# A new order table for an adaLN transformer block on one core: TensorE's instruction fetches enter the planner's transfer model

## The chip, the cores and the metric

The kernel runs on one core of one Trainium2 chip. The core has five engines with an instruction stream each: TensorE (PE in the profile; its weight loads are PEld), VectorE (DVE), ScalarE (ACT), GpSimd (POOL) and SyncE (SP), which here issues most of the DMAs. The metric is the device time of one execution in microseconds (us). Lower is better.

## The reference

A block of 2048 tokens of width 640 is computed: modulation vectors from a condition `c`, sliding-window attention (32 heads of 20, window 256) and a gated MLP of inner width 1536, each behind a LayerNorm and with a gate on its way back into `x`.

```python
mod = (_silu(c) @ w_mod).reshape(c.shape[0], 6, 1, -1)
sa, ca, ga, sb, cb, gb = (mod[:, i] for i in range(6))
h = _layernorm(x) * (1 + ca) + sa
qkv = h @ wqkv                                  # 32 heads of 20
scores = q @ k^T * 20 ** -0.5, masked to 0 <= i - j < 256
x = x + ga * (softmax(scores) @ v) @ wo
h = _layernorm(x) * (1 + cb) + sb
x = x + gb * ((_sigmoid(h @ w_gate) * (h @ w_up)) @ w_down)
```

## The kernel before

The tokens are cut into 8 chunks of 256 (two blocks of 128). A chunk a goes through these steps:

- **ln1**: two blocks of x are loaded (`load_x`). DVE takes their statistics (`bn_stats`, line 751), POOL takes the power -0.5 (lines 756 and 758), and DVE or POOL writes the normalised rows (lines 768 and 771). They are transposed into hT, by TensorE for chunks 0 and 1, by two transposing DMAs ("atr", issued by SP, line 778) for the others. Five "modulate" operations (one for each 128 columns; line 786 on ACT, 787 on DVE or POOL) multiply by 1 + ca and add sa.
- **qkv**: for each block and each of q and k, two matmul chains of 5 x 320 columns into a PSUM bank, two copies (lines 850 on ACT, 851 on DVE) into a staging tile stg of which there are four, and a transpose into QT or KT: by TensorE for chunks 0 and 1, by one transposing DMA of SP ("qkt") for the others. v needs the copies alone.
- **attention**: 12 score sets (6 in chunk 0). A set is a group of matmuls into the one score tile S (four PSUM banks), one exp of 128x2048 on ACT (line 971), and one or two masks on POOL (979, 981). After six sets their product with v (the lines 657 with M<-E,V) goes to two of the four PSUM banks of M; DVE transposes, divides and transposes back (1018 to 1027), four DMAs write the result to a DRAM tile doc, one DMA per half reads it back as oT.
- **outproj, mlp**: product with wo (its rows times the gate: five DVE or POOL multiplications "wos", line 1192), residual, second LayerNorm, two transposing DMAs ("btr") into h2T, five modulates, then the 12 gate and up chains, tanh on ACT, one DVE product each, and the product with wd.

The first stretch also loads all weights (q, k, v, wo, wg, wu, wd and w_mod) and computes the modulation vectors. For that a small matmul ("ctr") turns c into a column; DVE, ACT and DVE make silu(c) of it (lines 624, 625, 626 and 628, the last being the broadcast copy silubc); "modA" is the product with the first two sixths of w_mod in five steps as the five pieces of w_mod land. "warm" and "fill" are matmuls on zeros whose results nobody uses (lines 637 and 648).

**What sets the order.** The block is not scheduled by the compiler. `Prog.op` numbers 2102 operations as the program is built, each with the engines that may run it, its tiles and a duration. `PLAN` is one list of 2102 numbers: number // 5 is the operation, number % 5 the engine (0 PE, 1 ACT, 2 DVE, 3 POOL, 4 SP). `schedule` walks through the list, gives each operation to its engine's queue in that order, and computes a start time by a model. The modelled times reach the program in one way alone: where a tile needs one of several buffers, it takes the one that the model says is free first. `emit` then writes each engine's queue in order, with the semaphore waits that the dependences need. So an engine runs strictly in the table's order, and an operation that waits holds up all that stand behind it on its engine.

In `schedule`, DMAs go through one modelled pipe: `bw` is the time at which the pipe is free; a DMA starts at the earliest `dlat` after its issue, adds its `work`, and lands 0.83 us before `bw`. `MIXED` is added when transposing and plain DMAs follow each other. `QMAX` holds an issue back when the pipe is over 4.5 us behind.

Of the kernel before, what the change touches and what calls it, by code (L numbers as in the profile page):

```python
# [80 lines left out]
class Prog:  # L81
# [69 lines left out]
    def schedule(self):  # L151
        free = {e: 0.0 for e in ENGS}
        bw = 0.0
        lastturn = False
        order = {e: [] for e in ENGS}
# [37 lines left out]
        for code in PLAN:  # L193
            o, e = self.ops[code // 5], ENGS[code % 5]
            assert e in o.engs and all(d.done for d in o.deps), (o.tag, e)
            st = max(free[e] + (SWITCH if e == "pe" and o.mode != pemode else 0.0), o.tmin)
            for d in o.deps:
                st = max(st, d.end + (0.0 if d.eng == "pe" and o.engs == ("pe",) else d.lat))
            if e == "dve" and o.port:
                st = max(st, free["pool"])  # L200
# [20 lines left out]
            if o.isdma:  # L221
                turn = o.dlat > 3.0
                wait = bw - st - o.dlat
                bw = max(st + o.dlat, bw + (MIXED * min(1.0, wait) if turn != lastturn and wait > 0 else 0.0)) + o.work
                lastturn = turn
                o.end = max(bw - 0.83, st + dur)
                s = rr
                rr = (rr + 1) % NDMA
                dmacnt[s] += 16
                o.key, o.val = f"d{s}", dmacnt[s]  # L230
                if dmalast[s] is not None:
                    o.deps.append(dmalast[s])
                dmalast[s] = o
            else:
                o.end = st + dur
# [104 lines left out]
def c_pe(n):  # L340
# [4 lines left out]
    222, 263, 3, 33, 81, 62, 114, 91, 13, 89, 8, 265, 195, 202, 57, 206, 212, 217, 225, 104, 99, 109, 119, 230, 372,  # L345
    352, 367, 357, 377, 362, 383, 388, 392, 235, 240, 245, 250, 270, 280, 255, 397, 400, 67, 410, 420, 417, 290, 406,
    275, 426, 445, 129, 452, 285, 300, 310, 317, 430, 435, 458, 461, 442, 472, 477, 466, 124, 305, 295, 595, 495, 500,
    480, 485, 580, 507, 520, 492, 134, 23, 526, 139, 144, 149, 742, 585, 591, 38, 530, 535, 73, 541, 154, 510, 516,
    545, 550, 556, 560, 566, 600, 169, 610, 606, 630, 570, 1209, 1214, 747, 762, 757, 752, 767, 617, 635, 642, 576,
    620, 626, 48, 43, 1605, 1611, 773, 778, 645, 787, 660, 650, 782, 667, 680, 685, 790, 796, 657, 710, 692, 820, 827,  # L350
    78, 1620, 1237, 810, 1626, 817, 715, 722, 695, 700, 800, 806, 725, 730, 1222, 736, 1217, 1618, 830, 837, 174,
    1635, 1641, 159, 164, 179, 189, 349, 1514, 18, 53, 1633, 1227, 1232, 1242, 1100, 707, 670, 677, 840, 845, 855,
    1248, 851, 1253, 1267, 1122, 1107, 1705, 1711, 1648, 28, 1718, 1532, 324, 905, 910, 917, 890, 895, 1537, 870, 877,
    901, 860, 1720, 1726, 1542, 867, 1650, 1662, 1657, 194, 930, 937, 920, 1667, 1279, 1134, 1509, 940, 1735, 1258,
    1263, 945, 990, 880, 1733, 926, 995, 952, 334, 970, 1114, 1274, 1672, 887, 955, 960, 1741, 184, 976, 2785, 1677,
    339, 966, 1748, 1288, 1002, 1699, 1005, 1010, 1040, 1045, 344, 1126, 2791, 1020, 1026, 1017, 1517, 1522, 1527,
    1052, 1055, 2805, 2811, 1030, 1085, 1090, 1303, 2798, 1548, 1553, 1558, 1060, 1066, 1291, 1037, 1097, 1567, 1282,
    1750, 1563, 2823, 2825, 1762, 1340, 1757, 1767, 1297, 1070, 980, 1075, 2831, 986, 1772, 1175, 1197, 1082, 2845,
    2851, 1345, 1352, 2684, 1320, 1325, 1139, 1375, 2818, 1119, 1182, 1332, 2843, 1475, 1777, 1694, 1689, 1684, 2689,
    1574, 1390, 2865, 2871, 2838, 2863, 1380, 1387, 1480, 1355, 1152, 2858, 1360, 1486, 1367, 1157, 1395, 1402, 2878,  # L360
    1969, 2885, 1305, 2891, 2883, 1310, 1317, 2707, 1445, 1450, 1456, 1410, 1415, 2697, 1579, 1784, 2905, 1789, 1794,
    1799, 3279, 1374, 2692, 2702, 1422, 1460, 1465, 1472, 2911, 2803, 1596, 2898, 1425, 1430, 1437, 2903, 1591, 1490,
    1495, 1501, 1162, 1167, 1172, 2712, 2717, 2925, 2952, 1704, 2947, 1804, 1805, 1603, 2723, 2728, 2743, 1586, 1820,
    1825, 1810, 2748, 2931, 1581, 1189, 329, 3287, 1817, 1832, 1872, 1850, 1855, 2995, 1835, 1840, 1847, 3284, 1409,
    2495, 1867, 3001, 1862, 3302, 3292, 2500, 2480, 2506, 1339, 2485, 2492, 3015, 2530, 2565, 2550, 1444, 2535, 2542,
    1887, 2555, 3021, 2561, 2570, 2759, 3035, 2576, 2585, 2515, 2590, 1882, 2520, 2600, 1892, 2943, 2918, 2733, 2738,
    1877, 3008, 3297, 3013, 2938, 3041, 1898, 1903, 3053, 1954, 2605, 3055, 2665, 2957, 2670, 2923, 2754, 2766, 2771,
    2597, 3061, 2761, 2781, 2527, 2612, 2962, 1907, 2620, 2514, 2635, 2650, 2655, 2640, 1194, 1972, 2584, 2619, 2676,
    2778, 2625, 2549, 2631, 2647, 3380, 3386, 1912, 3195, 3200, 3180, 2662, 3160, 3185, 3191, 3028, 3207, 2967, 1919,
    3075, 1924, 3165, 3080, 3172, 3090, 3095, 3033, 3125, 3130, 3136, 3086, 3102, 3110, 3115, 3048, 4524, 4519, 3073,  # L370
    3068, 1201, 1936, 1946, 3398, 3307, 3312, 1149, 3393, 3122, 3400, 3145, 3215, 1932, 1941, 3422, 3406, 3318, 3323,
    3338, 1959, 1927, 1977, 3150, 1964, 3220, 3226, 3157, 2055, 2060, 2065, 3343, 1144, 4065, 2030, 2035, 3427, 4071,
    3245, 2040, 2017, 3260, 3265, 3271, 2022, 3432, 3437, 4078, 3250, 3257, 3442, 4085, 4091, 3328, 2002, 2007, 3230,
    2070, 2075, 2045, 2050, 2081, 2090, 4098, 2087, 2095, 2100, 2105, 2110, 4105, 2115, 2120, 2125, 2130, 2135, 2150,
    2155, 3235, 4111, 2160, 2141, 2147, 4125, 4131, 3354, 2989, 2974, 3464, 2175, 2180, 2165, 2170, 3449, 3242, 2185,
    2190, 2195, 2201, 4532, 2207, 2210, 2215, 4145, 2220, 2225, 2230, 4151, 2261, 2235, 2240, 2245, 2250, 2255, 2270,
    2275, 3333, 4083, 4118, 4103, 4123, 3418, 4143, 4138, 3413, 2267, 3144, 3349, 4158, 2280, 2979, 3459, 3454, 2984,
    3214, 2994, 3469, 1987, 1992, 2285, 2290, 2321, 4165, 4171, 3356, 2295, 2300, 2305, 2310, 2315, 2330, 2335, 2340,
    2345, 4187, 2327, 4235, 4241, 5749, 3500, 3505, 2350, 2381, 1983, 2027, 1997, 4192, 3512, 3515, 3520, 3527, 3470,
    4542, 3485, 4255, 4261, 2355, 3490, 2360, 3552, 2365, 3475, 2370, 2435, 2375, 3547, 4163, 3378, 5762, 3109, 3482,  # L380
    3497, 2387, 3371, 3179, 4248, 4253, 2013, 4268, 4273, 4197, 4202, 3557, 3366, 4275, 2410, 2390, 2415, 2440, 3362,
    4281, 4295, 2445, 2452, 4301, 4547, 2395, 4527, 4537, 4435, 2400, 4350, 4355, 4361, 2407, 5754, 4552, 3537, 4440,
    4330, 4335, 4341, 4385, 4610, 4616, 3532, 4288, 3542, 4390, 4293, 4178, 5757, 4183, 4308, 3563, 3568, 4447, 2420,
    3577, 2427, 4315, 4320, 4400, 4405, 3589, 5777, 5772, 5782, 4397, 4412, 4326, 4313, 4630, 3572, 3584, 4657, 4628,
    4636, 4365, 4370, 4455, 4470, 4475, 4481, 4558, 4563, 5767, 5788, 4460, 4466, 4567, 4572, 5793, 5295, 5301, 4377,
    3606, 5802, 4420, 4500, 4425, 4432, 4505, 4512, 4207, 4485, 4490, 4497, 3598, 3593, 5313, 5814, 5315, 5321, 2455,
    3602, 2460, 2465, 3615, 3620, 4648, 3611, 4652, 5328, 5335, 5341, 2472, 3640, 3645, 3650, 4662, 4667, 4672, 3625,
    3630, 3635, 3666, 3655, 3660, 3700, 5355, 5361, 3705, 3710, 3715, 3675, 3680, 3685, 3690, 3695, 3720, 3726, 3732,
    3672, 5375, 4214, 4454, 2479, 4219, 4224, 5333, 4689, 3735, 3740, 4229, 4694, 5381, 3745, 3750, 3755, 3786, 2434,
    3760, 3765, 3770, 3775, 3780, 4623, 5308, 5348, 4643, 4679, 5373, 5353, 4684, 3820, 3825, 3792, 5368, 5395, 5401,  # L390
    3830, 3835, 5797, 5417, 3795, 3800, 3805, 3810, 3840, 4584, 4579, 4699, 3815, 4234, 4598, 3855, 4419, 5809, 4384,
    3846, 5422, 5427, 5432, 3852, 5465, 5471, 3860, 3865, 4715, 4700, 4705, 4730, 4735, 4587, 5437, 5485, 4742, 5491,
    4712, 4720, 4727, 4762, 3870, 3875, 3880, 3906, 4745, 4593, 5413, 5828, 5483, 4603, 4750, 4757, 4782, 3885, 5498,
    5505, 5511, 5503, 3890, 3895, 3900, 3912, 3915, 4607, 5388, 3920, 3940, 3925, 3930, 3935, 5525, 4767, 5393, 3966,
# [61 lines left out]
TR1 = 2  # L456
NPH = 2
NPQ = 2
PQ = ()
KEEP = 3  # L460
DSAFE = 1.0
MIXED = 1.3
NPB = 0
OUTE = ("sp", "act")
XE = ("sp", "act")
MW = 64
AFTER = 1
NOW = 1
# [778 lines left out]
```

## Time and profile before

| what | us |
|---|---|
| three runs | 332.11, 332.77, 333.69 (median 332.77) |
| the profiled execution | 332.26 |
| its span, first to last instruction | 330.3 |
| outside the span | 1.96 |
| PE busy | 321.0 |
| ACT busy | 231.7 |
| DVE busy | 209.3 |
| POOL busy | 177.6 |
| PE's longest wait after the first 23 us, on a transposing DMA QT<-stg | 1.7 |

By the windows view, the DMA engines' share is 0.82 in the first 10 us, 0.94 to 1.15 in each stretch of 10 us from there to 80 us, and below 0.75 after that. An idle time of PE costs time only once: PE works with few interruptions from 11.47 us to the end, so whatever it waits is added to the total.

One thing about the rows of PE must be known. A matmul of 320 columns is shown 0.297 to 0.299 us long, but the next one starts 0.135 to 0.136 us after it. The shown end is modelled, so a wait of PE is about 0.16 us longer than the profile's bracket says.

### The profile page before, as it was taken

The numbers are of one execution on the slowest core, as the hardware profiler recorded it, in microseconds if no ns is written. First come the engines' busy times: TensorE is split into PE (matmuls) and PEld (weight loads), VectorE is DVE, ScalarE is ACT, GpSimd is POOL, SyncE is SP. The second block draws the span as 40 slices with busy tenths as digits, with TensorE's granted clock in tenths as the row PEclk, the third lists the DMA queues.
The fourth block names the chain that finished last, engine by engine and source line by source line (L and its number), as shares of the span: only waits on it lengthen the run. The fifth ranks groups of instructions, "written<-read, shape, count | busy, mean of one in ns | idle before, by whom it ended". The sixth has DMA issues, their size and how long they took to land.

```text
span 330.3 us, 10115 instructions
## 1 busy us (share of the span) xinstructions
PE 321.0 (97%) x4151; PEld 230.7 (70%) x4152; DVE 209.3 (63%) x431; ACT 231.7 (70%) x225; POOL 177.6 (54%) x271
## 2 busy tenths in 40 slices
PE   6999899799999999999999999999999999999996
PEld 2776566467776667766776776876786677878885
DVE  5699898678478767765665556454656384646323
ACT  1599989689887797867797977896887878111320
POOL 2257786674957583868565656537384829101100
DMA  7989999999770256568303303234031313112101
GB/s 249 374 315 304 299 191 203 182 186 260 143 122 0 42 124 130 114 91 136 91 6 78 75 19 66 58 90 89 2 79 46 96 20 85 38 46 44 58 0 60
DMA packets 72999, 38.07 MB, mean 115 GB/s; under 512 B 46586, under 2 KB 71674, under 8 KB 72954
## 3 DMA queue, kind: packets, MB, share of 16 engines
q1 hardware_dynamic: 71936, 36.29, 47.3%
q10 hardware_dynamic: 1018, 1.15, 1.1%
q8 instruction: 32, 0.52, 0.7%
q14 instruction: 13, 0.11, 0.1%
HBM read 21.30 MB, written 5.25 MB: 80 GB/s over the span
## 4 chain that ended last, share of the span: by engine, by line
PE 87%; DMA 4%; POOL 3%; DVE 2%; SPq 1%; issue 1%; ACT 1%; POOLq 0%; DVEq 0%
PE M L656 72%; PE S L657 8%; PE M L657 6%; DMA wd<-in_w_mod_dram 2%; DMA oT<-doc 1%; DMA hT<-x 1%; SPq L778 1%; POOL E L979 1%; ACT E L971 1%; POOL x L768 1%; PE S L656 0%; POOL E L981 0%; SPq L554 0%; POOL st L758 0%; DVE wo L1192 0%
## 5 line engine op out<-in xcount | busy, mean ns | idle before, releaser
L971 ACT ACTIVATE E<-S 128x2048 bf16<-128x2048 f32 x90 | 168.9, 1876 | 36.8 <-PE S L657 34.9
L979 POOL TENSOR_SCALAR_AFFINE_SELECT E<-E 128x512 bf16<-128x512 bf16 (+2 forms) x90 | 73.3, 827 | 43.1 <-DVE Tn L1025 18.4
L981 POOL TENSOR_SCALAR_AFFINE_SELECT E<-E 128x512 bf16<-128x512 bf16 (+1 forms) x84 | 65.8, 795 | 22.3 <-ACT E L971 11.1
L656 PE MATMUL M<-h2T,wu 128*128 128x256 bf16 x480 | 70.2, 273 | 0.0
L656 PE MATMUL M<-h2T,wg 128*128 128x256 bf16 x480 | 67.7, 273 | 0.0
L1148 DVE SCALAR_TENSOR_TENSOR hh<-sig,M 128x512 bf16<-128x512 f32 x48 | 32.5, 682 | 45.0 <-ACT sig L1146 27.6
L656 PE MATMUL M<-wd,hh 128*128 128x320 bf16 (+2 forms) x396 | 58.5, 295 | 0.0
L656 PEld LDWEIGHTS M<-h2T,wu 128*128 128x128 bf16 x480 | 44.5, 98 | 11.3 <-issue 3.8
L1146 ACT ACTIVATE sig<-M 128x512 f32<-128x512 f32 x48 | 28.5, 595 | 32.9 <-PE M L656 32.9
L656 PEld LDWEIGHTS M<-h2T,wg 128*128 128x128 bf16 x480 | 45.9, 98 | 8.0 <-issue 1.1
L656 PEld LDWEIGHTS M<-wd,hh 128*128 128x128 bf16 x396 | 37.2, 98 | 13.9 <-issue 0.8
L657 PE MATMUL S<-QT,KT 20*128 20x256 bf16 (+1 forms) x960 | 35.9, 245 | 0.2 <-ACT QT L850 0.2
L851 DVE CAST stg<-M 128x320 bf16<-128x320 f32 x44 | 20.9, 483 | 15.0 <-PE M L656 14.8
L1167 DVE TENSOR_TENSOR x<-M,x 128x320 bf16<-128x320 f32 (+2 forms) x33 | 15.3, 475 | 22.9 <-PE M L656 22.3
L751 DVE BATCH_NORM_STATS2 st<-x 128x6 f32<-128x320 bf16 x64 | 28.6, 478 | 1.2 <-DMA x<-in_A_x_dram 0.8
L656 PE MATMUL M<-wk,hT 128*128 128x320 bf16 x160 | 27.6, 300 | 1.1 <-DVE hT L787 0.9
L656 PE MATMUL M<-wq,hT 128*128 128x320 bf16 x160 | 26.5, 299 | 2.1 <-DMA QT<-stg 1.7
L1018 DVE STREAM_TRANSPOSE T<-M 128x512 f32<-128x512 f32 x32 | 21.6, 699 | 11.0 <-PE S L657 9.7
L657 PEld LDWEIGHTS S<-QT,KT 20*128 20x128 bf16 x960 | 14.0, 92 | 19.5 <-ACT E L971 13.3
L656 PE MATMUL M<-wv,hT 128*128 128x320 bf16 x160 | 26.7, 299 | 0.0
L656 PE MATMUL M<-wo,oT 128*128 128x320 bf16 x160 | 25.1, 300 | 0.3 <-DMA oT<-doc 0.3
L657 PEld LDWEIGHTS M<-E,V 128*32 128x32 bf16 x960 | 20.1, 97 | 4.2 <-issue 2.5
(79 smaller groups left out, 302.4 us busy)
## 6 DMA issues: line engine op xcount, KB each, us to landing
x<-in_A_x_dram SPq DMA_DIRECT2D x23, 160.0 KB
doc<-On SPq DMA_DIRECT2D x64, 40.0 KB
wd<-in_w_mod_dram SPq DMA_DIRECT2D x6, 320.0 KB
wd<-in_B_w_down_dram SPq DMA_DIRECT2D x4, 480.0 KB
out_dram<-x SPq DMA_DIRECT2D x11, 160.0 KB
wu<-in_w_mod_dram SPq DMA_DIRECT2D x5, 320.0 KB
oT<-doc SPq DMA_DIRECT2D x8, 192.0 KB
wg<-in_B_w_gate_dram SPq DMA_DIRECT2D x2, 576.0 KB
```

The costliest lines, as they stand in the source:

```text
L656: return e.matmul(o, l, r, start=st, stop=sp, skip_group_check=True)
L657: return e.matmul(o, l, r, start=st, stop=sp, tile_position=tp, skip_group_check=True)
L751: A("dve", lambda e, g, bi=bi, j=j: e.bn_stats(v(bi * 12 + j * 6, 6), src[bi].ap[:, j * 320:(j + 1) * 320]), 0.48, reads=[src[bi].r()], wr ...
L768: return e.tensor_scalar(dst[bi].ap[:], src[bi].ap[:], v(30 + bi, 1), v(32 + bi, 1), op0=ALU.mult, op1=ALU.add)
L851: return e.tensor_copy(dst(), src())
L971: A("act", lambda e, eng: e.activation(E.ap[:], Sp.ap[:], ACT.Exp, scale=SM_SCALE), 1.876, reads=[Sp.r()], writes=[E.r()], prio=3, tag=f"e ...
L979: return e.affine_select(ap, ap, pattern=[[0, ap.shape[1]], [1, 128]], compare_op=ALU.is_ge, fill=0.0, base=0, channel_multiplier=-1)
L981: return e.affine_select(ap, ap, pattern=[[0, ap.shape[1]], [-1, 128]], compare_op=ALU.is_ge, fill=0.0, base=-1, channel_multiplier=1)
L1018: A("dve", lambda e, g, h=h: e.transpose(T1.ap[:, 512 * h:512 * h + 512], X[h].ap), 0.694, reads=[X[h].r()], writes=[T1.r(h)], prio=3.5, t ...
L1146: A("act", lambda e, g, pg=pg, sg=sg: e.activation(sg.ap[:], pg.ap[:], ACT.Tanh, scale=0.5), c_act(512), reads=[pg.r()], writes=[sg.r()], ...
L1148: A("dve", lambda e, g, pu=pu, sg=sg, f0=f0: e.scalar_tensor_tensor(out=hh.ap[:, f0:f0 + 2, :], in0=sg.ap[:].rearrange("p (a b) -> p a b", ...
L1167: A("dve", lambda e, g, ps=ps, bi=bi, c0=c0, n=n: e.tensor_tensor(x1[bi].ap[:, c0:c0 + n], ps.ap[:, 0:n], x1[bi].ap[:, c0:c0 + n], op=ALU. ...
```

## The change

The operations, their durations and their dependences stay as they are. Three things change: the transfer model in `schedule`, the table `PLAN`, and two constants (`MIXED` from 1.3 to 0.3, and the new `FETCH`, the times of 32 instruction fetches).

```diff
+        nf = 0
...
                 turn = o.dlat > 3.0
                 wait = bw - st - o.dlat
+                low = max(bw - 0.83, st + 0.5) - 0.5
                 bw = max(st + o.dlat, bw + (MIXED * min(1.0, wait) if turn != lastturn and wait > 0 else 0.0)) + o.work
+                if o.work >= 1.1 and st > 10:
+                    bw = max(bw, st + 4.98)
+                while nf < len(FETCH) and FETCH[nf] <= bw - 1.03:
+                    if FETCH[nf] >= low:
+                        bw += 0.85
+                    nf += 1
                 lastturn = turn
-                o.end = max(bw - 0.83, st + dur)
+                land = bw - 0.83
+                if land < 7.2 and o.work > 0.1:
+                    land += 0.2 if land < 3.6 else 0.6 if land < 5.4 else 0.4 if land < 6.2 else 0.15
+                o.end = max(land, st + dur)
...
 PLAN = [
-    222, 263, 3, 33, 81, 62, 114, 91, 13, 89, 8, 265, 195, 202, 57, 206, 212, 217, 225, 104, 99, 109, 119, 230, 372,
+    222, 23, 225, 230, 81, 114, 263, 91, 3, 53, 89, 8, 265, 235, 58, 195, 240, 202, 206, 212, 372, 245, 250, 99, 104,
...
-MIXED = 1.3
+MIXED = 0.3
+FETCH = [
+    15.05, 23.29, 29.7, 39.76, 44.68, 54.89, 67.15, 76.75, 88.25, 93.9, 107.75, 113.95, 124.1, 133.35, 142.45, 151.5,
...
```

The two tables hold the same 2102 operations. PE keeps its 975. ACT has 227 in place of 232, DVE 432 in place of 431, POOL 262 in place of 259, SP 206 in place of 205. Of the operations that change engine, 20 are copies of q and k (14 from DVE to ACT, 6 from ACT to DVE), 10 copies of v (7 from ACT to DVE), 39 modulates (13 from ACT to POOL, 7 from POOL to DVE, 6 from ACT to DVE and 6 from DVE to ACT among them), 11 plain DMAs between SP and ACT. The score sets keep their places among PE's operations to within a handful of positions. What is moved most, read off the tables by operation:

| queue | order before | order after |
|---|---|---|
| PE, start | modA (ones), ctr, six warm, modA 0, modA 1, warm, three transposes of x, modA 2, ... | two warm, modA (ones), warm, ctr, four warm, modA 0, fill, modA 1, fill, modA 2, modA 3, three transposes, ... |
| DVE, start | c_col, siluc, silubc, four bn_stats, ... | c_col, siluc, two bn_stats, silubc, aggregate, two bn_stats, ... |
| SP, 23 to 40 us | wm3 (half), x7, wg, wm2 (half), atr of chunk 2 (one), wu, x6, wg, gate out, atr of chunk 2 (other), wo, wg, ... | x6, x7, wm2 (half), wg, wm3 (half), gate out, wm3 (half), both atr of chunk 2, wo, wu, gate in, x8, ..., wg, ... |
| SP, 47 to 73 us | x10, KT of chunk 2, both oT of chunk 0, gate out, wg, x11, QT, QT, KT of chunk 2, atr of chunk 4, wd, atr of chunk 4, QT, gate in, QT, KT, KT of chunk 3, both btr of chunk 0, ... | oT of chunk 0, x10, gate out, oT, QT, KT, QT, KT of chunk 2, wd, gate in, wu, both atr of chunk 4, QT, QT, KT, KT of chunk 3, both btr of chunk 0, wg, ... |
| ACT, 23 to 53 us | copies of q, k and v and one or two modulates between the exps, two copies ahead of the exp at 33.39, five operations ahead of the exp at 52.97 | the first exp at 23.23 followed at once by the next, two copies ahead of the third, two ahead of the exp at 33.39, six operations ahead of the one at 52.97; x11's load is issued here |
| DVE, near 28 us | two bn_stats of chunk 3, then the two transposes that free M; the other two bn_stats after 34 us | all four bn_stats of chunk 3, then those transposes |
| PE, near 76 us | after the product with v at 73.53: two chains of q and v of chunk 4 (10 matmuls), then the first up chain of the MLP | the up chain's first two matmuls come first, then those 10, five more of v and a score set, then the rest of the up chain |

## The prediction

> **What bounds the kernel now.** I read the page first, then the waits of PE, then PE's timeline around each wait, then SP and the chain of waits.
>
> ```profile
> PE 321.0 (97%) x4151; PEld 230.7 (70%) x4152; DVE 209.3 (63%) x431; ACT 231.7 (70%) x225; POOL 177.6 (54%) x271
> PE   6999899799999999999999999999999999999996
> ```
>
> PE is the bound: after the start it falls below nine tenths only in slices 5 and 8 (33 to 41 and 58 to 66 us). A new order of the same operations can win what PE waits, and nothing else. The waits of PE between 23 and 73 us are all there is after the start:
>
> ```profile
> PE M L656 <- DMA QT<-stg: 1.7, 1, 1.7
> PE M L656 <- DVE hT L787: 0.9, 1, 0.9
> PE M L656 <- DMA oT<-doc: 0.3, 1, 0.3
> PE M L656 <- DVE T L1018: 0.3, 1, 0.3
> PE S L657 <- ACT QT L850: 0.2, 1, 0.2
> ```
>
> With the 0.16 us that a modelled end hides, PE's timeline makes them 1.91 (to 60.32), 1.05 (to 39.14), 0.43, 0.43 and 0.32, 4.1 in all. Two holes at 68 us add 0.55 (a score group ends later than the next start allows; seven matmuls at 68.37 take 1.42 where 6 x 0.136 + 0.30 = 1.12 would do). That is **4.7 us to be won**.
>
> The windows view says what else is full there (columns: stretch, busy us of PE, PEld, DVE, ACT, POOL, clock, DMA share, GB/s):
>
> ```profile
> 20.00:30.00 10.00, 9.73 (x173) 6.47 (x170) 9.42 (x24) 9.55 (x11) 7.25 (x14) 1.00 0.95 263
> 30.00:40.00 10.00, 8.93 (x139) 5.79 (x139) 8.85 (x19) 9.93 (x12) 7.28 (x10) 1.00 1.15 311
> 50.00:60.00 10.00, 8.30 (x136) 5.29 (x134) 8.31 (x19) 8.99 (x10) 7.37 (x12) 1.00 1.03 180
> 180.00:190.00 10.00, 10.00 (x119) 7.10 (x117) 6.32 (x11) 9.53 (x10) 5.67 (x9) 1.00 0.35 85
> ```
>
> From 20 to 40 us ACT has no room: where PE's wait goes there, the exps are late next. From 50 us on ACT has a tenth free. Late in the kernel PE is full and the DMAs idle.
>
> SP's timeline shows what the longest wait hangs on:
>
> ```profile
> 51.54 0.44 SPq L554 DMA_DIRECT2D wg<-in_B_w_gate_dram  x1
> 52.03 0.46 SPq L554 DMA_DIRECT2D x<-in_A_x_dram  x1
> 53.02 3.45 SPq L778 DMA_TRANSPOSE QT<-stg  x2
> 56.61 1.35 SPq L778 DMA_TRANSPOSE KT<-stg  x1
> 58.13 2.03 SPq L778 DMA_TRANSPOSE hT<-x  x1
> 60.91 1.21 SPq L778 DMA_TRANSPOSE hT<-x  x1
> ```
>
> The second QT transpose is issued at 54.36 (2.11 of the 3.45) and lands at 60.0; the staging tile that it reads is the one PE needs at 58.4. Ahead of it stand a piece of wg (landed 55.7) and x11 (56.1). A transposing issue takes 1.21 to 1.35 us alone, 2.03 and 2.11 with the pipe full.
>
> **The change, part by part** (my sum starts from the profiled execution, 332.26, of which 330.3 is span; the median of the three runs lies 0.51 above it).
>
> The transfer model emits nothing. It acts through the table and the choice of buffers. No operation is added or removed, so busy times move only between engines: a copy of q or k costs 0.48 on DVE (483 ns a row) and 0.44 on ACT.
>
> *Start, 0 to 23 us: 0.* PE now begins with two warm pairs, which wait only for DVE's memset (ends 1.25) and not for POOL's ident (PE's first row is at 2.17). Cold matmuls of 512 columns are 0.427 apart, so ctr, behind three pairs and modA's ones, starts at about 1.3 + 3 x 0.85 + 0.38 = 4.2 in place of 2.55. From ctr to siluc's start 0.77 passes now (2.55 to 3.32), so siluc stands at 5.0, and DVE, in order, holds the first bn_stats behind it (4.51 now). With silubc (0.49, less the usual 0.08) between the statistics, the normalised x is some 0.95 late: TensorE's transposes of x at 9.4, not 8.45. Against that, all of modA but the last step now runs before them, and the last step ends at about 10.3, as now (10.38). Then come mA, the modulates and the first projection, at 11.5 as now (11.47). Ends: -0.5 (the last copy early) and +0.95 (nothing hides it).
>
> *23 to 52 us: -0.9.* Both transposes of chunk 2 now go out together, ahead of wo, wu and a piece of wg. Now the second is issued at 30.48 behind those and lands at 35.45. I put it at 29.6, landing 33. The modulate that PE waited for at 39.1 stood on DVE behind the normalisation of chunk 3 (38.37), which waited for POOL's power (37.62); it is now on ACT, and POOL's power stands earlier. The hole of 1.05 goes. But next late is ACT. From the exp at 23.23 to the one at 52.97 are eleven exps of 1.88. The gap between two is at least 0.5 (41.75, 44.13, 46.52: 2.38 apart), which hides one copy; in the new order three gaps hold more, about 0.8, 0.9 and 2.4. Sum: 23.23 + 11 x 1.88 + 8 x 0.5 + 4.1 = 52.0. So at most 0.95 is won, and I take 0.9. The holes of 0.43 and 0.32 near 30 us stay: DVE has two more bn_stats (0.9) in front of the transposes that free M. Ends: -1.8 (all three holes) and +0.5 (M freed 0.5 later sets PE back).
>
> *The wait for oT: -0.3.* The oT DMAs are no longer behind a KT transpose (48.04, 1.69 us of SP), but PE comes 0.9 earlier and the five wo multiplications end at 52.38 now, two DVE operations earlier then. Of 0.43 I keep 0.1. Ends: -0.43 and +0.5 (wo late by one DVE copy).
>
> *The wait at 58 us: -1.7.* The four q and k transposes of chunk 2 now go out one behind the other, with neither wg nor x11 between, x11 on ACT's queue. At 1.3 an issue from 48 on, the last is out by 53.5 and lands by 57, the staging tiles free in turn from 52. PE asks for the second at about 56.5. I leave 0.2 of the 1.91. Ends: -1.91 and 0.
>
> *The holes at 68 us: -0.5.* Chunk 4's two transposes are issued at 58.13 and 60.91 and land at 61.6 and 64.9; five ACT modulates and copies then run back to back to 69.4. They now follow wd, gate in and a piece of wu; POOL's rows (54.84 and 57.32) let them go out at about 56 and 57.5. Four of the five ACT operations are elsewhere. Ends: -0.55 and +0.5.
>
> *New: a wait for h2T of chunk 0, +0.8.* After the product with v at 73.53 the first up matmuls stood behind 10 projection matmuls (10 x 0.136 = 1.36) and started at 76.67. Now they are in front. PE would come at 75.36 - 3.4 = 72.0. The two btr transposes are issued at 68.26 and 69.57, land at 71.1 and 73.1, and modulates run to 75.5. SP loses wg and x11 (0.9) and the slow issues (0.8 each) ahead of them, so I move this chain 2.6 earlier: first modulates done at 71.8 to 72.8. Ends: 0 and the full 3.4.
>
> *wg's second piece*, once landed at 55.7, now goes out behind btr, at about 68, landing by 71; PE needs it at about 74. Margin 3, no cost.
>
> *From 80 us to the end: 0.* PE is full in every row and DMA share is 0.04 to 0.72; the last chains, copies and the last store are the same. Ends: -0.3 and +0.5 (a queue head that waits).
>
> Sum: 0 - 0.9 - 0.3 - 1.7 - 0.5 + 0.8 = -2.6, so 329.7 from this execution and 330.2 from the median. I take **329.9 us**.
>
> A row of q8 bears on the premise: 32 packets of 16 KB are TensorE's instructions, each 0.93 to 1.8 us on one DMA engine, one at 58.16 while the late transpose is in flight. The Trainium skill, page "Runtime: NRT & Kernel Launch", section "Instruction fetch mechanics", says that crossing a block of 16 KiB costs one tail bump of a DMA, mostly hidden. For PE itself the trace agrees (none of its waits is put down to a fetch); what a fetch does to a transfer beside it, the Trainium skill does not say.
>
> **Rivals.**
>
> *Given back.* The holes to 68 us close, but h2T of chunk 0 comes no earlier than now: first modulates done at 75.4, PE goes on at 75.6. The old path reached the same matmuls at 76.67, 1.36 of it other work, so 75.31. That is +0.3: 332.6. For it: POOL, DVE and SP form one chain through residual, statistics and transposes, each in order. Against: SP is back to back from 50 to 73 us and loses 0.9 + 1.6 of that. With half of it, 331.3.
>
> *Fetches hide anyway.* If the 0.85 per fetch is not real, the new model is no truer than the old, and the new order is one of many with equal stalls elsewhere: 332.3. For it: no wait of PE is put down to a fetch. The rule of the Trainium skill above would have it so too. Against: queue positions change for the better whatever the fetches do.
>
> *Slower.* Place: SP, 53 to 70 us. The new order puts wd and a piece of wu directly ahead of eight transposing issues (chunk 4, QT and KT of chunk 3, both btr). If each then takes 2.07 as the two slow rows do, in place of 1.28, SP is 8 x 0.79 = 6.3 later. From my start at about 55 for the first, the last is out at 55 + 8 x 2.07 = 71.6, against 70.84 now, and lands with the modulates 0.8 later than now; with PE's other waits of the same kind (projections of chunk 4) 1.0 more, and 0.3 as above: 332.26 + 2.1 = 334.4. It decides once more than six of the eight are slow. Against: only two of eight transposing issues between 53 and 70 us are slow now.
>
> **How the numbers follow.** Forecast (holes close, 328.2 to 331.0): 0.55. Given back: 0.17, at 331.2 to 333. Hidden fetches: 0.08, at 332.3. Slower: 0.17, at 334.4. All 4.7 and more won, 327.3: 0.03. A measurement of this kernel tells about 0.5%, 1.7 us, from no change. So faster 0.58, same 0.25, slower 0.17. The likeliest case's own range is 328.2 to 331.0. The range that should hold 8 in 10 takes in the given-back and hidden cases and the lower half of the slower one: 327.8 to 333.9.
>
> **What would show it.** In PE's waits: no row for QT<-stg and none for hT; in their place one on h2T near 72 us. In SP's timeline: no plain load between the four chunk 2 transposes, which end by 54 us. On ACT: the twelfth exp from 23 us on starts near 52.0. In PE's row of slices, nines in slice 8. If the wait for QT<-stg is there again, or PE's waits before 80 us sum to 4 or more, the prediction is wrong.

## The result and the profile after

Six runs of the kernel after took 329.43 us in the median (328.90 to 329.78), six of the kernel before 332.70 (332.11 to 333.69). The ratio is **0.9899, with a 95% interval of 0.9881 to 0.9917**. Measured once more beside the last experiments, it was 329.48 against 331.93, 0.9929 (0.9911 to 0.9947). The profiled execution took 329.54, of which 327.8 is span: 2.72 less than that of before, 2.5 of it in the span; the traces below can explain that much, and not the 3.27 between the medians. 329.9 had been predicted.

The page of the kernel after, PE's busy time and its row of 40 slices:

```profile
PE 322.6 (98%) x4152; PEld 231.2 (71%) x4152; DVE 206.9 (63%) x432; ACT 229.1 (70%) x221; POOL 178.3 (54%) x274
PE   8999999999999999999999999999999999999996
```

Slices 5 and 8 are nines now. PE's waits of the kernel after between 11 and 80 us (us in total, times, longest):

```profile
PE M L672 <- ACT hT L802: 0.5, 2, 0.3
PE M L672 <- DVE hT L803: 0.3, 1, 0.3
```

These are all: QT<-stg (1.7), hT from DVE (0.9), oT and T are gone. Lines stand 16 lower in the file after, so L672 is L656 of before, L794 is L778, L987 is L971. The windows view of after (columns as before):

```profile
30.00:40.00 10.00, 9.79 (x175) 6.48 (x177) 9.97 (x23) 9.71 (x10) 7.63 (x12) 1.00 1.01 264
...
50.00:60.00 10.00, 9.78 (x154) 6.31 (x151) 8.92 (x23) 8.94 (x12) 7.67 (x14) 1.00 1.03 204
60.00:70.00 10.00, 9.61 (x90) 5.99 (x87) 8.19 (x20) 7.70 (x8) 5.73 (x9) 1.00 1.16 196
```

PE gained 0.86 us of work from 30 to 40 and 1.48 from 50 to 60. The queue behind the second gain is SP's (timeline of after, 47 to 70 us; start, length, engine, line, operation):

```profile
48.12 1.26 SPq L794 DMA_TRANSPOSE QT<-stg  x1
49.42 2.33 SPq L794 DMA_TRANSPOSE KT<-stg  x1
51.79 1.31 SPq L794 DMA_TRANSPOSE QT<-stg  x1
53.64 1.24 SPq L794 DMA_TRANSPOSE KT<-stg  x1
54.94 0.57 SPq L570 DMA_DIRECT2D wd<-in_B_w_down_dram  x1
55.64 0.41 SPq L570 DMA_DIRECT2D gbc<-gate  x1
56.09 0.43 SPq L570 DMA_DIRECT2D wu<-in_B_w_up_dram  x1
56.64 4.20 SPq L794 DMA_TRANSPOSE hT<-x  x2
60.95 2.65 SPq L794 DMA_TRANSPOSE QT<-stg  x2
```

The four q and k transposes of chunk 2 go out between 48.12 and 54.88 with no load between them. The second QT is issued 2.57 earlier than before (54.36) and its last part lands at 55.12, not 60.19.

Where the 2.5 us of the span went is seen best when each trace is cut at three places: the first projection matmul, and the first matmul of the product with v of 64 matmuls in its first and second occurrence (PV1, PV2). All times are from the traces, in us; "to the end" is from PV2 to the last instruction.

| kernel | first projection | PV1 | PV2 | projection to PV1 | PV1 to PV2 | to the end |
|---|---|---|---|---|---|---|
| before | 11.47 | 51.08 | 73.53 | 39.61 | 22.45 | 256.7 |
| after | 11.65 | 50.28 | 71.06 | 38.63 | 20.78 | 256.8 |
| difference | +0.18 | -0.80 | -2.47 | -0.98 | -1.67 | 0.0 |

From 71 us to the end the two kernels take the same time, though their tables differ there as well. All of the gain is made by 71 us, in two stages.

### The profile page after: what moved, and what is told of

Same layout as the page of the kernel before. It is cut to its first block, busy times and chain, and to the rows that moved or that the text cites. A ratio compares the mean times of both kernels' runs of the same rounds, so it can differ in the third digit from the quotient of the medians.

```text
span 327.8 us, 10118 instructions
## 1 busy us (share of the span) xinstructions
PE 322.6 (98%) x4152; PEld 231.2 (71%) x4152; DVE 206.9 (63%) x432; ACT 229.1 (70%) x221; POOL 178.3 (54%) x274
## 4 chain that ended last, share of the span: by engine, by line
PE 79%; ACT 1%; DVE 0%; issue 0%
PE M L672 66%; PE S L673 7%; PE M L673 6%; ACT E L987 1%; DVE x L1183 0%
## 5 line engine op out<-in xcount | busy, mean ns | idle before, releaser
L987 ACT ACTIVATE E<-S 128x2048 bf16<-128x2048 f32 x90 | 168.9, 1877 | 37.9 <-PE S L673 36.6
L995 POOL TENSOR_SCALAR_AFFINE_SELECT E<-E 128x512 bf16<-128x512 bf16 (+2 forms) x90 | 74.4, 835 | 36.3 <-ACT E L987 20.9
L672 PE MATMUL M<-h2T,wu 128*128 128x256 bf16 x480 | 70.4, 273 | 0.0
L672 PE MATMUL M<-h2T,wg 128*128 128x256 bf16 x480 | 68.2, 273 | 0.0
L672 PE MATMUL M<-wd,hh 128*128 128x320 bf16 (+2 forms) x396 | 57.7, 295 | 0.0
L672 PEld LDWEIGHTS M<-h2T,wu 128*128 128x128 bf16 x480 | 44.0, 98 | 11.1 <-issue 3.8
L672 PEld LDWEIGHTS M<-h2T,wg 128*128 128x128 bf16 x480 | 45.9, 98 | 7.8 <-issue 1.5
L672 PEld LDWEIGHTS M<-wd,hh 128*128 128x128 bf16 x396 | 37.2, 98 | 14.8 <-issue 1.1
L672 PE MATMUL M<-wk,hT 128*128 128x320 bf16 x160 | 28.2, 300 | 0.3 <-ACT hT L802 0.3
L672 PE MATMUL M<-wv,hT 128*128 128x320 bf16 x160 | 28.2, 300 | 0.0
L672 PE MATMUL M<-wq,hT 128*128 128x320 bf16 x160 | 26.7, 299 | 0.4 <-DVE hT L803 0.3
L672 PE MATMUL M<-wo,oT 128*128 128x320 bf16 x160 | 24.6, 299 | 0.2 <-ACT hT L802 0.2
L867 DVE CAST stg<-M 128x320 bf16<-128x320 f32 x36 | 17.1, 484 | 11.0 <-PE M L672 10.6
L772 POOL TENSOR_SCALAR st<-st 128x2 f32<-128x2 f32 x16 | 3.6, 228 | 36.4 <-DVE st L769 33.0
```

The costliest lines, as they stand in the source:

```text
L672: return e.matmul(o, l, r, start=st, stop=sp, skip_group_check=True)
L772: A("pool", lambda e, g: e.tensor_scalar(v(28, n), var(), EPS, None, op0=ALU.add), 0.2, reads=[st.r(("m", bi)) for bi in range(n)], writes ...
L867: return e.tensor_copy(dst(), src())
L987: A("act", lambda e, eng: e.activation(E.ap[:], Sp.ap[:], ACT.Exp, scale=SM_SCALE), 1.876, reads=[Sp.r()], writes=[E.r()], prio=3, tag=f"e ...
L995: return e.affine_select(ap, ap, pattern=[[0, ap.shape[1]], [1, 128]], compare_op=ALU.is_ge, fill=0.0, base=0, channel_multiplier=-1)
```

## The experiments

**Three mixed tables: where the gain is made.** PLAN is the new table up to an operation of the first or the second large product with v, then the old order of what is left (h1, h2), or the old up to there and then the new (h3). The rest is the kernel after. A mixed table also changes buffers: of the 771 tiles, 124 to 219 get another one than in after, 213 to 351 another than in before. The hand edits further below (s1, t1, t2, f1, c1, c2) leave every tile in the buffer that it has in before, and f2 in that of after.

```diff
-PLAN = new
+PLAN = new[:k] + [c for c in old if c // 5 not in done]   # h1: k at 50 us; h2: k at 71 us
+PLAN = old[:k] + [c for c in new if c // 5 not in done]   # h3: k at 71 us
```

> The new table up to the first product with v of chunk 1 (about 50 us), the old order for all that is left. Theory (the gain comes in stages: 0.8 by that product, where the exp chain on ACT sets the pace, 1.7 at the staging tiles near 58 us): the product with v of 64 matmuls starts at about 50.3 in place of 51.1, and since the loads of wg and x11 are again ahead of the transposes of q and k, most of the 58 us hole is back. Total 331.9 against 332.7, between 331.4 and 332.5. Rival (the gain is spread over the whole table, or made after 71 us): less than 0.3 here, 332.4 or more.

> The new table up to the second product with v of chunk 1 (about 71 us), the old order from there. Theory: everything that is won is won by then, so 329.4 to 330.2. Rival (the late part of the new table carries a part of the gain): halfway, 331 or more.

> The mirror image: old order up to the second product with v of chunk 1, the new table from there. Theory: PE has no waits to lose after 75 us, so the time is that of before, 332.2 to 333.0, and the product with v starts at about 73.5. Rival: 331.5 or less.

Measured against the kernel before at 332.55: h1 332.04, ratio 0.9981 (0.9958 to 1.0004); h2 329.69, 0.9918 (0.9898 to 0.9938); h3 332.60, 1.0019 (0.9992 to 1.0045). The new order up to 71 us alone wins what the whole table wins, and the new order behind 71 us alone wins nothing. (The profiled execution of h3 was its slowest, 335.17: PE waited 2.6 us for hT near 41 us, and PV1 and PV2 came at 55.15 and 76.50, where about 73.5 had been expected. From PV2 to the end it took 256.9, about as before.) In h1, PE's waits between 11 and 90 us begin with

```profile
PE M L672 <- DMA QT<-stg: 1.7, 1, 1.7
```

The old wait is there again, but the gain of the first stage (PV1 at 50.32) passes it: PE goes on at 59.30, 1.02 earlier than before (60.32). It is lost right behind. The windows view of h1, and for comparison of before, for the 3.4 us after the wait (the number behind POOL's is the clock):

```profile
59.40:62.80 3.40, 3.40 (x17) 1.65 (x19) 1.49 (x6) 0.44 (x1) 0.70 (x2) 0.50 1.06 233
60.30:63.70 3.40, 3.38 (x30) 2.20 (x31) 1.88 (x8) 1.82 (x3) 1.02 (x3) 1.00 0.87 201
```

From 59.42 to 62.83 TensorE's granted clock was half, which costs about 1.7 us (an estimate: half of 3.41), and PV2 came at 73.71, against 73.53 before. The mean granted clock of this execution is 0.995, as in two others of h1's six (332.31, 332.70 and 332.81 us). The three at 1.000 took 330.27, 331.63 and 331.78, where the ten executions of before at 0.999 or more have a median of 332.4. So the 0.8 of the first stage seems to reach the end where the clock stays full; three executions are few.

**Only the longest wait taken away.** In the kernel before, wg's piece and x11 leave the queue ahead of the QT transposes. One statistics operation of x11 on DVE (660) follows it.

```diff
-    ..., 1581, 1189, 329, 3287, ...     # wg piece (SP)
+    ..., 1924, 329, 3165, ...           # behind the transposes of h2T
-    ..., 1847, 3284, 1409, ...          # x11 (SP)
+    ..., 1444, 3284, 2535, ...          # behind chunk 2's KT
```

> Before, with three places changed and no others: the second piece of wg goes out behind the two h2T transposes of chunk 0, x11 behind the four q and k transposes of chunk 2, and one bn_stats of x11 on DVE goes down to its sister. Theory (the 58 us hole hangs on what stands ahead of the second QT transpose on SP and in the DMA pipe): that transpose lands about 1.7 earlier, PE's wait on QT<-stg falls from 1.7 to 0.5 or less, and 1.2 to 1.7 of it reach the end: 331.0 to 331.5. Rival (given back at the next late thing, hT of chunk 4 or h2T of chunk 0): the wait goes, the total stays at 332.4 or more.

Measured: 332.28, ratio 0.9993 (0.9971 to 1.0016), so nearly nothing; nearer to "given back". The trace shows that the wait for QT<-stg was gone, yet PV1 was at 53.44, 2.36 late. So PE asked for the staging tile at 60.44 only, and the missing wait alone, or PV1 to PV2 (20.37, before 22.45), proves little. The landing does: the second QT transpose, issued at 54.28 (before 54.36), landed at 57.58 and not at 60.19. The timeline of PE in this run has, near 41 us:

```profile
42.86 0.25 PE L657 MATMUL M<-wd,silubc 128*32 128x160 bf16 x4 [1.72 <-DMA wd<-in_w_mod_dram]
```

This is the second half of wm3, the last piece of w_mod, issued here at 35.02 and landed at 42.81. In the first profile it had landed at 40.25, a quarter of a microsecond before PE's use at 40.50. Nothing that this edit moves stands ahead of it. In six profiles of the old order it landed between 40.25 and 43.04.

**Only the hole at 38 us taken away.** In the kernel before, the modulate that PE waits for goes from DVE to ACT (t1); with it a copy of v from ACT to DVE (t2).

```diff
-    ..., 1567, 1282, 1750, ...          # modulate of chunk 2, DVE
+    ..., 1066, 1281, 1291, ...          # on ACT, ahead of ACT's next modulate
-    ..., 1060, 1066, 1291, ...          # t2: copy of v, ACT
+    ..., 2825, 1067, 1762, ...          # on DVE
```

> The kernel before, with one modulate of chunk 2 (the one for which TensorE waits 0.9 at 39.1) moved from DVE to ACT, ahead of ACT's next modulate. Theory (ACT's exps are the next late thing up to 52 us): the wait on DVE's hT goes, but ACT has no room, the exp that begins at 52.97 begins no earlier, and the time falls by at most 0.5 to about 332.1. Rival (the wait of TensorE is what counts): the whole 1.05 is won, 331.5.

> The kernel before, with the same modulate moved to ACT and one copy of v moved from ACT to DVE. Theory: ACT is relieved by the copy, the exps come earlier, and about 0.85 is won: 331.7. Rival: the same as with the modulate alone.

Measured against 332.06: t1 332.03, ratio 1.0004 (0.9988 to 1.0020), t2 332.51, 1.0001 (0.9979 to 1.0024). Neither wins anything that the intervals can show, which is within "at most 0.5" for t1 and a miss for t2. The rival of t1 is out; that of t2 (the same as with the modulate alone) came true. But the reason is not the one given, ACT. PE's timeline of t1 where the hole was:

```profile
39.40 0.45 PE L656 MATMUL M<-wk,hT 128*128 128x320 bf16 x2 [0.27 <-ACT hT L786]
39.68 0.43 PE L656 MATMUL M<-wv,hT 128*128 128x320 bf16 x2
40.49 0.40 PE L656 MATMUL M<-ident,stg 128*128 128x128 bf16 x4 [0.37 <-DVE T L1018]
40.73 0.57 PE L656 MATMUL M<-wv,hT 128*128 128x320 bf16 x3
41.29 0.25 PE L657 MATMUL M<-wd,silubc 128*32 128x160 bf16 x4
```

Next late is DVE's transpose that frees M (true hole 0.54), and right behind it the second half of wm3, which landed at 41.24 and is used at 41.29. Three things were late by almost the same amount. Projection to PV1 took 39.52 in t1 and 39.61 before.

**Fetches moved.** Each warm operation becomes 16 matmuls of 64 columns. The columns stay, TensorE has 196 more instructions (matmuls and weight loads), and its instruction packets fall elsewhere. f1 is the kernel before with this, f2 the kernel after.

```diff
-        for k in range(2):
-            ins = e.matmul(p_S.aps[0][:, 3, :], Eall[:, 0, 0:128], Eall[:, 0, 128:640], ...)
+        for k in range(16):
+            ins = e.matmul(p_S.aps[0][:, 3, 0:64], Eall[:, 0, 0:128], Eall[:, 0, 128:192], ...)
```

> The kernel before, with each warm-up operation of TensorE as 16 matmuls of 64 columns instead of 2 of 512: the same columns, 196 more instructions, so TensorE's instruction stream crosses each block of 16 KB some 60 instructions (2.5 to 2.9 us) later: the fetch at 58.16 goes to about 61, the one at 47.62 to about 50. Theory (a fetch holds a transposing issue and its transfer that lie beside it by about 0.85): the slow issue of hT at 58.13 (2.03) becomes 1.2 to 1.35, the slow ones are found where the fetches now lie, and the time may move by up to 1 us in either direction with the waits. Rival (a long queue of transfers makes the issues slow, fetches hide): the same issues stay slow, time as before within 0.3 us.

> The kernel after, with the same edit of the warm-up operations. Theory of the fetch: the slow issues of after (hT 41.00 at 2.17, KT 49.42 at 2.33, hT 57.89 at 2.94) become 1.2 to 1.35, others beside the moved fetches become slow. If the new table is good only for the fetch times that its model was given, the time rises by 0.5 us or more over after (330 and above); if it is good whatever the fetches do, it stays within 0.4 us of after.

Measured: f1 334.09, ratio 1.0064 (1.0039 to 1.0089), so 2 us slower, where up to 1 had been expected; f2 330.05, 0.9938 (0.9914 to 0.9962). In f1 the packets came at 52.94 and 63.10 instead of 47.62 and 58.16, some 5 us later and not 2.5 to 2.9. SP's timeline of f1:

```profile
53.12 3.25 SPq L778 DMA_TRANSPOSE QT<-stg  x2
56.51 1.23 SPq L778 DMA_TRANSPOSE KT<-stg  x1
57.91 1.20 SPq L778 DMA_TRANSPOSE hT<-x  x1
...
59.85 1.21 SPq L778 DMA_TRANSPOSE hT<-x  x1
...
63.12 2.12 SPq L778 DMA_TRANSPOSE QT<-stg  x1
```

The hT issue at 57.91 takes 1.20, not 2.03, and the QT issue at 63.12, which took 1.24 before, takes 2.12 beside the moved packet. The second QT transpose, issued at 54.69, lands at 58.45, 3.76 us later; in the kernel before, with the packet at 58.16 in its way, it took 5.83. PE has no wait for QT<-stg at all in f1, though wg's piece and x11 stand ahead of the transpose as before. All 14 traces can be sorted by these two things (us from the issue of chunk 2's second QT transpose to the landing of its last part):

| | a packet starts between issue and landing | none does |
|---|---|---|
| wg's piece and x11 ahead | 5.33 to 5.83 (before, h1, h3, t1, t2) | 3.76 (f1) |
| neither ahead | 4.97 (f2) | 3.25 to 3.33 (after, its second profile, h2, s1, c1, c2, c3) |

So a packet in the way is worth 1.6 to 2.1 us, twice the 0.85 of the model, and the two loads about half a microsecond (f1 and f2 are one trace each). In the five traces with both, the transpose landed 2.0 to 2.1 us after the packet's start, whenever it had been issued. But now the packet at 63.10 is in the way of hT, issued at 59.85, which lands at 65.44 (before: issued at 60.91, landed at 64.94), and ACT, in order, holds an exp behind it:

```profile
65.47 1.09 ACT L786 ACTIVATE hT<-hT,mA 128x256 bf16<-128x256 bf16 x2 [2.63 <-DMA hT<-x]
```

PE's hole moved from 58.4 (1.91) to 66.0 (2.33). So a fetch does not hide from the transfer beside it, and the rival falls. The 2 us of time are for the most part something else: the score group behind the hole starts at 68.37, only 0.49 later than before (67.88), but from there to PV2 f1 takes 7.21 and before 5.65. The windows view of f1 behind the hole:

```profile
69.20:72.60 3.40, 3.26 (x14) 1.80 (x14) 1.64 (x2) 2.80 (x5) 3.40 (x5) 0.51 0.70 149
```

As in h1, the granted clock was half for 3.41 us (69.24 to 72.65), about 1.7 us by the same estimate; the mean granted clock of all four executions of f1 is 0.994 or 0.995.

In f2, PV1 to PV2 took 20.41 (after: 20.78) and its ratio, 0.9938, lies within the interval that after has in the last experiment (0.9911 to 0.9947). Two of the three slow issues of after became 1.33 and 1.35; the one at 41.00 still took 1.47, with a packet still at 41.13. The new order holds with moved fetches too.

All 14 traces together say the same of the issues. Of SP's transposing issues that had a TensorE packet under way at their start or starting within 1.2 us of it, 80 of 149 took over 1.5 us; of the others 11 of 579.

**The same by hand, with wm3.** c1 is the kernel before with wg's piece and x11 behind and the second half of wm3 ahead of wo; c2 has the modulate on ACT as well.

```diff
-    ..., 1045, 344, 1126, ...           # wm3, second half
+    ..., 1274, 344, 1672, ...           # behind chunk 2's second atr, ahead of wo
```

> The kernel before with wg's piece and x11 behind (as in the run that moved these two alone), and the second half of w_mod's last piece (wm3) issued ahead of wo instead of at 34.39. Theory: in the run without the move of wm3 its late landing (42.8, where TensorE asked at 41.1) ate the gain at 58 us; with wm3 landed by about 39 the 1.9 us of the wait for QT<-stg reach the end: about 1.9 below the kernel before, and TensorE has no row for wd<-in_w_mod_dram near 41 us. Rival (the gain at 58 us is given back elsewhere, whatever wm3 does): within 0.5 us of the kernel before.

> The same, and the modulate of chunk 2 moved from DVE to ACT as well. Theory: the modulate was worth nothing by itself because wm3 landed at 41.24 and DVE's transposes of M came 0.53 late; with wm3 early, DVE's transposes are left, so 0.3 to 0.6 more is won: 2.2 to 2.5 below the kernel before. Rival (ACT is next late at 38 us): nothing more than the run without the modulate.

Measured against 331.93: c1 330.84, ratio 0.9961 (0.9947 to 0.9975), which is 0.8 to 1.8 us; c2 331.11, 0.9972 (0.9954 to 0.9991). wm3 landed at 38.3 and 36.9, and PE has no wait for it. So wm3 is part of the answer, and the whole 1.9 is not won: PE's waits in c1 are now

```profile
PE M L656 <- DVE hT L787: 0.8, 1, 0.8
PE S L657 <- ACT E L971: 0.5, 1, 0.5
PE M L656 <- DMA oT<-doc: 0.4, 1, 0.4
```

and ACT's timeline of c1 tells where the rest went:

```profile
63.94 1.09 ACT L786 ACTIVATE hT<-hT,mA 128x256 bf16<-128x256 bf16 x2 [0.99 <-DMA hT<-x]
64.94 1.85 ACT L971 ACTIVATE E<-S 128x2048 bf16<-128x2048 f32 x1
66.69 1.08 ACT L786 ACTIVATE hT<-hT,mA 128x256 bf16<-128x256 bf16 x2
67.68 0.74 ACT L850 ACTIVATE V<-M 128x320 bf16<-128x320 f32 x2
68.31 1.87 ACT L971 ACTIVATE E<-S 128x2048 bf16<-128x2048 f32 x1
```

Between the exps at 64.94 and 68.31 stand two modulates and two copies. In after the same pair of exps starts at 64.88 and 67.24, since those operations stand elsewhere, though hT of chunk 4 lands hardly earlier there (63.86 and 63.91). The modulate of c2 is worth nothing again: PV1 comes 0.44 earlier than in c1 (0.26 of it from the start), PV2 0.22 later, behind hT of chunk 4, which lands at 64.13.

**The old start, and after again.** c3 is after with all that stands ahead of the first projection in the old order (330 of the 771 tiles get another buffer); the other is the kernel after once more.

```diff
-PLAN = new
+PLAN = old[:69] + [c for c in new if c // 5 not in done]
```

> The kernel after with the start of the table before (all that stands ahead of the first projection). Theory A (the start was a gain: before's order asks for the first piece of w_mod just as it lands, after's does other work meanwhile): first projection anywhere from 11.5 to 12.4 in place of 11.65 to 11.69, time 0.3 above after. Theory B (the shown profiles: the start is a loss of 0.2 to 0.3): first projection 11.47, time 0.25 below after.

> The kernel after once more, beside the others on their chip: 0.990 of the kernel before, 329.4. If the run of after with moved fetches (0.994) was slower by more than chance, this run stays at 0.990.

Measured: c3 329.55 (328.71 to 330.92), ratio 0.9920 (0.9903 to 0.9937), after 329.48 (328.92 to 330.48), 0.9929 and not the 0.990 that was expected of it. The times of the two cannot be told apart. c3's first projection was at 12.33. Over all profiles, the old start has it at 11.47, 11.59, 11.84, 11.85, 11.89, 12.07, 12.10, 12.33 and 12.36, the new one at 11.65 to 11.69 in all five.

The three stages of the runs that the argument rests on:

| kernel | first projection | PV1 | PV2 | projection to PV1 | PV1 to PV2 |
|---|---|---|---|---|---|
| h1 | 11.69 | 50.32 | 73.71 | 38.63 | 23.39 |
| h2 | 11.69 | 50.32 | 70.90 | 38.62 | 20.58 |
| h3 | 11.84 | 55.15 | 76.50 | 43.31 | 21.36 |
| s1 | 12.10 | 53.44 | 73.81 | 41.34 | 20.37 |
| t1 | 12.36 | 51.88 | 73.79 | 39.52 | 21.91 |
| t2 | 11.89 | 51.52 | 73.73 | 39.63 | 22.21 |
| f1 | 12.07 | 51.64 | 75.58 | 39.57 | 23.94 |
| f2 | 11.65 | 50.27 | 70.69 | 38.62 | 20.41 |
| c1 | 11.85 | 51.33 | 72.50 | 39.48 | 21.17 |
| c2 | 11.59 | 50.88 | 72.72 | 39.30 | 21.83 |
| c3 | 12.33 | 50.95 | 72.36 | 38.62 | 21.41 |
| after again | 11.65 | 50.27 | 70.96 | 38.62 | 20.68 |

Before, t1 and t2 have the old queue of SP in this stage. They reach PV1 up to 0.80 us apart and PV2 within 0.26, since the second QT transpose landed at 60.19, 60.32 and 60.31, each time behind a packet at 58.16 to 58.31. That is no fixed time, however: in h1, with PE 0.98 earlier, the packet came at 57.05 and QT landed at 59.16.

## Why the prediction was right, point by point

The time, 329.9, was within 0.5 of the result. The largest term came out as worked out, and its mechanism (the order of SP's queue) holds, but only half of it was named: the wait took the packet at 58.16 as well, which the prediction saw and did not price. Some terms were mis-sized, and that they cancelled is luck: PV2 was to come 3.4 earlier and came 2.5 earlier, and the 0.8 set against it for h2T wasn't needed.

- *Start, 0*: +0.18 in the two profiles. The transposes of x came at 9.43, as worked out (9.4). What the step missed is that the old start is not one number. It waits for a piece of w_mod (in t1 it landed at 8.27, modA began at 8.31) and is 11.47 only in the luckiest of nine profiles; their median is 11.89. So beside the new 11.67 the start is rather a gain of 0.2. c3 did not settle that in time.
- *23 to 52 us, -0.9*: -0.98, and the exp predicted at 52.0 began at 52.16. In all six runs with the new order here (c3 too) the stage takes 38.62 or 38.63, with ACT's exps following one another; that ACT sets the new end of this stage fits all of them. For the old order the step named one cause, the modulate on DVE. There were three (modulate, M's transposes, wm3), as t1 and t2 showed, and the new table moves them all: wm3's second half is issued at 26.96 and lands at 31.6. The prediction's rows did not price wm3, though the table of the change lists it in the order of SP. The holes of 0.43 and 0.32 near 30 us, which were to stay, fell to 0.14 or less.
- *The wait for oT, -0.3*: 0. The hole is 0.38 (0.43 before), and 0.67 in the second profile of after. oT's last part landed 0.96 earlier (52.09, before 53.05), hardly more than PE came earlier.
- *The wait at 58 us, -1.7*: the score group behind it came 2.49 earlier, 0.80 of which is from PV1; -1.69. Shown by h1 (the wait stays with the old queue, 1.87 in PE's timeline), by c1 and c2 (no wait without the two loads, with PE there at 58.8 and 58.3) and by f1 (no wait with the loads in place and the packet elsewhere). The prediction put the slow issues of 2.11 and 2.03 down to a full pipe. The one of 2.03 moved with the packet (f1), and the longest in after, 2.94 at 57.90, stands beside a packet at 57.93. The one of 2.11, at 54.36, has no packet near it, and took 1.34 and 1.33 in t1 and t2; its cause stays open.
- *The holes at 68 us, -0.5*: nothing is won there in after itself (holes of 0.45, 0.16 and 0.27). c1 showed another use of the moved ACT operations: without that move, 1.0 us more stands between two exps, and part of the gain at 58 us is lost again.
- *The wait for h2T, +0.8*: +0.14. The h2T transposes are issued at 66.40 and 67.73, 1.85 earlier than before, and the first up matmul starts at 72.87, with 75.36 - 2.5 = 72.9 as the time at which PE came there. The chain itself was as predicted (first modulates done at 72.7, between 71.8 and 72.8); PE was the later one.
- *From 80 us, 0*: 0.0.

Of the rivals, *given back* did not happen in after, but is what happened to t1 and c2, where the modulate alone was moved. *Fetches hide anyway* fell by f1. The Trainium skill, page "Runtime: NRT & Kernel Launch", section "Instruction fetch mechanics", has the crossing of a block mostly hidden; for TensorE itself every trace here agrees (no wait of PE is put down to a fetch), for a transposing DMA beside it f1 and f2 show 1.6 to 2.1 us. What that rival had right is that the new order does not need the fetches where its model puts them (f2). *Slower* needed six slow issues of eight between 53 and 71 us; there was one.

What stays open: how much of the gain comes from knowing the fetch times at all. f2 shows that the order is good without them being right; whether a table found without them would be as good was not tried. That the ACT chain is what bounds the new first stage is read from the profiles, not tested by itself. What makes the clock fall to half was not tested either. And the size of the gain is known only to be between 0.5% and 1.2%: the two comparisons gave 0.9899 and 0.9929.

## What to carry to other kernels

A wait that is taken away is worth only the distance to the next late thing, so before pricing it, list everything that would arrive within a microsecond behind it: transfers with their landing times, and other engines' work. Steps that uncover each other pay together and not one by one (t1 alone paid nothing, c1 0.4%, the whole table 0.7 to 1.0%). Before a longer time is put down to a wait, look at the granted clock: in h1 and f1 a stretch at half clock cost more than the wait ahead of it had changed. Cut the trace at a few fixed instructions and compare stage by stage over several profiles, since a load that lands just in time in one execution is 2 us late in the next.

## What the runs showed of the hardware

- A fetch of 16 KB of TensorE's instructions slows a transposing DMA beside it. Over the 14 traces such an issue took over 1.5 us, up to 2.9, in 80 of 149 cases, in place of 1.2 to 1.35, and chunk 2's second QT transpose landed 1.6 to 2.1 us later with a packet in its way.
- The parts of one plain load can land far apart. In s1, from wo on, the first of the 16 parts landed 2.3 us before the last (38.19 and 40.46), in the kernel before within 0.07. No run here shows why.
- After a long wait TensorE's clock can fall to half for 3.41 us. In three traces it did, 0.1, 0.9 and 1.8 us after the end of a wait of 1.7 (h1), 2.2 (f1) and 2.6 (h3); in no trace did it fall elsewhere between the start and the last matmul. Waits of 1.4 to 1.75 in before, s1, t1 and t2 had no such stretch in their profiles. Beside the experiments the kernel before ran 55 times: 7 executions have a mean granted clock of 0.995 or less and took 333.6 to 334.9, all others at most 333.3. Of the 31 executions with the new order up to 71 us (after twice, f2, h2, c3) none has less than 0.999. So the waits that the new table takes away seem to cost more, now and then, than their length.
- The clock's rise is not tied to the first matmul. With the same instructions, 512-column matmuls changed from 0.427 to 0.216 us apart between 5.2 and 7.3 us in the old start (first PE row at 2.17 in all), and between 4.7 and 7.0 us in the new one (1.30 or 1.31 in all). The Trainium skill, page "TensorE: Matmul & The Clock Gate", Part 1, says that the window is free-running, and gives a variation of 500 ns in one sentence and a changing count of cold matmuls in the next. The traces agree with the second: 2.3 us between two runs of the same start. It cost nothing here, since the first projection of the new start came at 11.65 to 11.69 in all of them.
